# Where the maxima of w_out and the stored copies of w_in stand in the first mixer of a four-layer kernel

## The chip, the core and the metric

The kernel runs on one core of a Trainium2 chip. The metric is the device time of one execution in microseconds; a version's time is the median of its runs. Five engines work side by side, each through its own list of instructions in order: TensorE (PE; its weight loads are shown apart as PEld), VectorE (DVE), ScalarE (ACT), GpSimd (POOL) and SyncE (SP), which issues every DMA here. They wait for each other through semaphores.

## The reference

x is 2048 x 640. Two layers alternate twice: an attention with a compressive memory (A, 32 heads, four segments), and a gated mixer (B) over 2048 positions. Only B of the first pair is touched by the change.

```python
x = x + A(layernorm(x), wq, wk, wv, wo, beta)
x = x + B(layernorm(x), w_in, w_sp, b_sp, w_out)
x = x + A(...)          # the same weights again
x = x + B(...)

def B(x, w_in, w_sp, b_sp, w_out):          # w_in 640 x 1728, w_sp 2048 x 2048, w_out 864 x 640
    z = gelu(x @ w_in)
    z1, z2 = z[:, :864], layernorm(z[:, 864:])
    g = w_sp @ z2 + b_sp[:, None]
    return (z1 * g) @ w_out
```

## The kernel before

Matrix products are made in float16 with every factor split into a high and a low part, so each product is three matmuls (high x high, high x low, low x high). A factor is scaled by a power of two taken from its largest element before it is split; that needs its maximum first.

One layer pair runs in three phases. Phase 1a is the attention. Phase 1b (`phase1b`) makes z1 and z2 of the mixer, 16 row tiles of 128 positions. Phase 2 (`phase2`; `phase2s` in the second pair) makes the spatial product with w_sp and the output.

**Phase 1b of the first pair.** The loop runs over an index i = 0 to 15; index i handles row tile `ts[i]`, in the order 0 to 7, 12 to 15, 8 to 11. The attention's output projection of tiles 0 to 11 is done in phase 1a; tiles 12 to 15 are projected here (`attn_out`, line 311, tile `yp`), at the head of indices 7 to 10, one index ahead of their use, from a transposed tile `o` (line 299). For each tile x is normalised, split into high and low halves (`xnhl`) and turned by a transposing DMA into `th` (line 252). PE multiplies `th` with the second half of w_in (`wi1`, giving z2) and then with the first half (`wi0`, giving z1), 30 matmuls each (`zp`, line 334). z2 is normalised and split into `zh`, `zl`, which stay on the chip; z1 goes to DRAM (line 348). There are two buffers of `th`, so a tile's `th` is issued soon after PE has finished the tile two before it, and has to be there one tile later.

**What else the loop carries.** `keep()` (line 148) stores the split halves of w_in to DRAM for the second pair, two DMAs of 1080 KB for `wi1` and two for `wi0`. The generator `more` (`other_scales`, lines 203 to 222) finds the maximum of w_out: seven loads (`wmst`), seven reductions (`wap`), a reduction to one column (`wam`), its store (`wmax`), a load that broadcasts it (`wmall`) and a last reduction (`pw`). One `next(more)` takes one such step; twelve end it. Both stand behind that index's z2 norm on DVE and its z1 store on SP (`issue_after`), nothing else ties them.

**Phase 2.** Row tile t of w_sp is loaded (`wr`, one buffer, line 678), its row maxima found (`am`, line 684), scaled and split by column halves (`wn`, lines 700 and 701), turned by two transposing DMAs into `wt` (line 702) and multiplied with `zh`, `zl` (`gp`, line 713, 96 matmuls, from row tile 0 on, with the tiles of the last indices last). The product is gated with z1 (`cz`), scaled, split and turned (`un`, `ut`) and multiplied with w_out (`cyp`, line 745, called a tail here), one product later. PE's order is product 0, product 1, tail 0, product 2, tail 1 and so on. The loads and splits of w_out (`wst`, `wuh`, `wul`, lines 130, 90, 91) stand on ACT and DVE ahead of the first gate. The row tiles 0 and 1 are prepared ahead of the loop: `behind(10)` to `behind(14)` put their DVE and ACT steps behind the z2 of indices 10 to 14.

**What sets the order.** In phase 1b only PE's order is that of the code; a scheduler places the other engines' instructions, by priority and by when the buffers they need come free. The buffers of phase 2 lie where those of phase 1b lay: that of `wr` over buffers of x, `o` and the staging tiles of w_out's maxima. From the loop of `phase2` on, the order of PE, SP, DVE and ACT is that of the code.

Of the kernel before, what the change touches and what calls it, by code (L numbers as in the profile page):

```python
# [267 lines left out]
def phase1b(g, o_d, x, x1_d, z1_d, put, after, w0=None):  # L268
    nc, tc = g.nc, g.tc
    zs = ZS if w0 is None else ZB  # L270
    with ExitStack() as ctx:
# [18 lines left out]
        def load(t):  # L290
            if t < NWO:
                x1 = pe2.tile([128, D], F32, tag="x1", name="x1")
                nc.sync.dma_start(x1, x1_d[t])
                return (x1,)
            xt = px2.tile([128, D], F32, tag="xt", name="xt")
            nc.sync.dma_start(xt, x[t])
            o = px1.tile([128, 2, KD, 128], F16, tag="o", name="o")
            d = o_d[t // 4][(t % 4) * 128:(t % 4 + 1) * 128]
            nc.sync.dma_start(o.rearrange("p i k c -> p (i k) c"), d.rearrange("p i c -> p (i c)"), transpose=True)
            return xt, o[:, 0], o[:, 1]  # L300

        def attn_out(t, *a):
            if t < NWO:
                x1 = a[0]
            else:
                xt, oh, ol = a
                yp = py.tile([128, 2, 512], F32, tag="yp", name="yp")
                for k in range(KD):
                    for j, (a, b) in enumerate(((oh, woh), (oh, wol), (ol, woh))):
                        for n in range(2):  # L310
                            nc.tensor.matmul(yp[:, n, :320], a[:, k, :], b[:, k, n * 320:(n + 1) * 320],
                                             start=(k == 0 and j == 0), stop=(k == KD - 1 and j == 2))
                x1 = pe2.tile([128, D], F32, tag="x1", name="x1")
                nc.vector.scalar_tensor_tensor(x1.rearrange("p (n c) -> p n c", n=2), yp[:, :, :320], g.yw,
                                               xt.rearrange("p (n c) -> p n c", n=2), ALU.mult, ALU.add)
                nc.sync.dma_start(x1_d[t], x1)
            xn = x1 if t < NWO else xt
            layernorm(g, x1, xn, D, 2, XS)
            return xn

        def xn_t(xn):
            th = pe2.tile([128, 2, KD, 128], F16, tag="th", name="th")
            hl = pe1.tile([128, 2, D], F16, tag="xnhl", name="xnhl")
            split_t(g, hl, th, xn)
            return th[:, 0], th[:, 1]

        def w_in_half(i, th, tl):
            zp = (pz0, pz1)[i].tile([128, 2, 512], F32, tag=f"zp{i}", name=f"zp{i}")
            wh, wl = wi[i]
            for k in range(KD):  # L330
                for j, (a, b) in enumerate(((th, wh), (th, wl), (tl, wh))):
                    for n in range(2):
                        c = n * FHH
                        nc.tensor.matmul(zp[:, n, :FHH], a[:, k, :], b[:, k, c:c + FHH],  # L334
                                         start=(k == 0 and j == 0), stop=(k == KD - 1 and j == 2))
            return zp

        def z2_half(t, zp):
            z2 = p1.tile([128, FH], F32, tag=f"z2{t % 2}" if w0 is not None else "z2", name="z2")
            i = nc.scalar.activation(z2.rearrange("p (n c) -> p n c", n=2), zp[:, :, :FHH], AF.Gelu_apprx_tanh, scale=g.zi[1])  # L340
            j = layernorm(g, z2, z2, FH, 2, zs)
            put(t, z2, p1)
            return i.ins, j.ins

        def z1_half(t, zp):
            z1 = p2.tile([128, FH], F32, tag="z1", name="z1")
            nc.scalar.activation(z1.rearrange("p (n c) -> p n c", n=2), zp[:, :, :FHH], AF.Gelu_apprx_tanh, scale=g.zi[0])
            return nc.sync.dma_start(z1_d[t], z1).ins
# [16 lines left out]
        for i, t in enumerate(ts):  # L365
            if i + 1 < NT:
                xn = attn_out(ts[i + 1], *a)
            last = z2_half(t, w_in_half(1, *th))
            g.mark[i] = last
            if i + 2 < NT:  # L370
                a = load(ts[i + 2])
            th1 = xn_t(xn) if i + 1 < NT else None
            sent = z1_half(t, w_in_half(0, *th))
            th = th1
            with tc.issue_after(last[1]), tc.issue_after(sent):
                if w0 is None and i in (3, 6):
                    g.wi[i == 3].keep()
                if i > 2:
                    next(more, None)


# [1193 lines left out]
def interleaved_layers(ctx, tc, x, wq, wk, wv, wo, beta, w_in, w_sp, b_sp, w_out, out):  # L1575
# [25 lines left out]
    for i in range(2):  # L1601
        z1_d = [dram(f"z1_{i}_{t}", (128, FH)) for t in range(NT)]
        with ExitStack() as zs:
            with ExitStack() as top:
                phase1a(g, att[i], top)
                if i:
                    ats.close()
                    w0 = zs.enter_context(tc.tile_pool(name="w0", bufs=1, reuse_waits="tile")).tile([128, 2, 7 * D], F16, name="w0")
                zp = zs.enter_context(tc.tile_pool(name="z2", bufs=1, reuse_waits="tile"))
                if i:  # L1610
                    zb = [zp.tile([128, 2, NT // 2, FHH], F16, name=f"zb{j}") for j in range(7)]
                    phase1b(g, o_d[i], xs[i], x1_d[i], z1_d, blocks(g, zb), att[i].after, w0)
                else:
                    zh = zp.tile([128, NT, FH], F16, name="zh")
                    zl = zp.tile([128, NT, FH], F16, name="zl")
                    phase1b(g, o_d[i], xs[i], x1_d[i], z1_d, whole(g, zh, zl), att[i].after)
            if i:
                phase2s(g, w_sp, x1_d[i], z1_d, zb, w0, xs[i + 1])
            else:
                phase2(g, w_sp, x1_d[i], z1_d, zh, zl, xs[i + 1], att[1])  # L1620
# [26 lines left out]
```

## Time and profile before

| what | before |
|---|---|
| median of 3 runs | 2313.51 us (2311.42 to 2315.06) |
| profiled execution, its own time | 2322.67 us |
| span in that profile | 2321.0 us |
| PE busy | 2169.7 us (93%) |
| DVE, ACT, POOL busy | 1506.6, 1175.5, 973.9 us |
| DMA queue of SP | 347.19 MB, 57.1% of 16 engines' span |
| mean granted clock of PE | 0.983 |

The profile records one execution; its times are used below as durations and places, and they are counted from the span's start. The first pair's phase 1b runs from about 639 to 837 us, its phase 2 from 839 to about 1250 us. In a row of the timeline stand start, duration, engine, source line, operation, written and read tiles, count, and in brackets how long the engine had sat idle before it and what ended that.

### The profile page before, as it was taken

The numbers are of one execution on the slowest core, as the hardware profiler recorded it, in microseconds if no ns is written. First come the engines' busy times: TensorE is split into PE (matmuls) and PEld (weight loads), VectorE is DVE, ScalarE is ACT, GpSimd is POOL, SyncE is SP. The second block draws the span as 40 slices with busy tenths as digits, with TensorE's granted clock in tenths as the row PEclk, the third lists the DMA queues.
The fourth block names the chain that finished last, engine by engine and source line by source line (L and its number), as shares of the span: only waits on it lengthen the run. The fifth ranks groups of instructions, "written<-read, shape, count | busy, mean of one in ns | idle before, by whom it ended". The sixth has DMA issues, their size and how long they took to land.

```text
span 2321.0 us, 50425 instructions
## 1 busy us (share of the span) xinstructions
PE 2169.7 (93%) x20487; PEld 1296.1 (56%) x20487; DVE 1506.6 (65%) x2812; ACT 1175.5 (51%) x1462; POOL 973.9 (42%) x726
## 2 busy tenths in 40 slices
PE   4889899999899979999999988999998999999999
PEld 2455565656555535555654555656665555555555
DVE  7588878787744545454434788787776767546454
ACT  3388788787632222121113797888875434322321
POOL 2188788888610100000001688889896323000000
PEclk9999999999899989999999999999999999999999
DMA  5543635455655357878656336354456434877875
GB/s 162 146 102 106 165 91 131 109 157 125 162 146 163 105 156 203 243 182 223 189 145 160 70 97 168 86 125 120 124 162 176 108 95 110 248 220 195 224 212 127
DMA packets 512008, 350.41 MB, mean 151 GB/s; under 512 B 409952, under 2 KB 447712, under 8 KB 506656
## 3 DMA queue, kind: packets, MB, share of 16 engines
q1 hardware_dynamic: 511776, 347.19, 57.1%
q8 instruction: 160, 2.62, 0.5%
q14 instruction: 72, 0.59, 0.1%
HBM read 161.10 MB, written 97.93 MB: 112 GB/s over the span
## 4 chain that ended last, share of the span: by engine, by line
PE 49%; DVE 4%; ACT 4%; DMA 2%; issue 2%; POOL 1%; SPq 0%; ACTq 0%; DVEq 0%; POOLq 0%
PE gp L713 11%; PE zp L334 7%; PE cyp L548 3%; PE cyp L745 3%; PE ga L499 3%; PE gb L499 3%; PE vps L1094 2%; PE pv L1370 2%; PE yps L1127 2%; PE ge L499 2%; PE gd L499 2%; PE gc L499 2%; PE kps L1151 1%; PE mp L1317 1%; PE qps L1151 1%
## 5 line engine op out<-in xcount | busy, mean ns | idle before, releaser
L1344 POOL TENSOR_TENSOR PL<-P,PH 128x1280 f16<-128x1280 f32 x248 | 649.9, 2623 | 159.9 <-ACT PH L1343 144.6
L1333 DVE TENSOR_REDUCE mx<-mp 128x2 f32<-128x1024 f32 (+3 forms) x512 | 408.4, 817 | 95.1 <-PE mp L1289 92.8
L1326 ACT ACTIVATE P<-es,sc 128x1024 f32<-128x1024 f32 (+1 forms) x384 | 370.4, 965 | 126.4 <-PE es L1289 123.3
L1343 ACT CAST PH<-P 128x1280 f16<-128x1280 f32 x256 | 320.3, 1253 | 18.5 <-PE pv L1370 11.8
L238 POOL TENSOR_TENSOR lnrs<-lnve,mhalf 128x1 f32<-128x1 f32 x92 | 56.0, 618 | 586.9 <-DVE lnve L237 585.7
L334 PEld LDWEIGHTS <-th 128*128 128x128 f16 x1920 | 188.1, 98 | 170.3 <-DMA th<-xnhl 6.5
L713 PE MATMUL gp<-zh,wt 128*128 128x432 f16 x1024 | 233.4, 348 | 12.6 <-DMA wt<-wn 12.6
L713 PEld LDWEIGHTS <-wt 128*128 128x128 f16 x1536 | 150.7, 98 | 144.3 <-DMA wt<-wn 14.2
L1317 PEld LDWEIGHTS <-qk 60*128 60x128 f16 (+1 forms) x2048 | 91.9, 93 | 224.4 <-issue 161.5
L499 PEld LDWEIGHTS <-wt 128*128 128x128 f16 x1344 | 131.5, 98 | 112.6
L1317 PE MATMUL es<-qk 64*128 64x512 f16 (+3 forms) x1024 | 134.9, 299 | 41.4 <-ACT P L1326 29.1
L1317 PE MATMUL mp<-qk 60*128 60x512 f16 (+3 forms) x1024 | 137.6, 306 | 34.1 <-DVE mx L1333 32.7
L1289 PEld LDWEIGHTS <-big 64*128 64x128 f16 x3072 | 141.2, 95 | 49.8 <-issue 2.5
L1370 PE MATMUL pv<-vs,PH 128*128 128x41 f16 x2560 | 168.2, 182 | 0.1
L1370 PE MATMUL pv<-vs,PL 128*128 128x41 f16 x2560 | 163.9, 181 | 4.0 <-POOL PL L1344 3.7
L1094 PE MATMUL vps<-wvh,xt 128*128 128x320 f16 x640 | 152.1, 303 | 4.5 <-DVE vs L1100 3.5
L334 PE MATMUL zp<-wi1h,th 128*128 128x432 f16 x640 | 149.5, 349 | 6.5 <-DMA th<-xnhl 5.2
L1370 PEld LDWEIGHTS <-PH 128*128 128x128 f16 x2560 | 142.5, 96 | 18.4
L1370 PEld LDWEIGHTS <-PL 128*128 128x128 f16 x2560 | 142.9, 96 | 5.7 <-POOL PL L1344 4.6
L713 PE MATMUL gp<-zl,wt 128*128 128x432 f16 x512 | 136.1, 348 | 0.0
L1151 PE MATMUL kps<-xt,wkh 128*128 128x512 f16 x380 | 121.9, 388 | 7.6 <-DVE phl L1185 7.3
L726 DVE TENSOR_TENSOR u<-u,cz 128x864 f32<-128x864 f32 x16 | 17.0, 1060 | 161.7 <-ACT u L724 111.8
(260 smaller groups left out, 4389.8 us busy)
## 6 DMA issues: line engine op xcount, KB each, us to landing
wr<-in_B_w_sp_dram SPq DMA_DIRECT2D x32, 1024.0 KB
qk<-st SPq DMA_DIRECT2D x256, 120.0 KB
x<-x SPq DMA_DIRECT2D x56, 320.0 KB
z<-z SPq DMA_DIRECT2D x32, 432.0 KB
cz<-z SPq DMA_DIRECT2D x32, 432.0 KB
turned<-wt SPq DMA_DIRECT2D x24, 512.0 KB
wt<-turned SPq DMA_DIRECT2D x24, 512.0 KB
st<-qhl SPq DMA_DIRECT2D x40, 256.0 KB
```

The source lines that it names most:

```text
L334: nc.tensor.matmul(zp[:, n, :FHH], a[:, k, :], b[:, k, c:c + FHH], start=(k == 0 and j == 0), stop=(k == KD - 1 and j == 2))
L499: nc.tensor.matmul(o[:, :FHH], wt[:, x, m, :], zb[b][:, y, m, :], start=start and i == j == 0, stop=i == NP - 1 and j == 2, skip_group_che ...
L713: nc.tensor.matmul(gp[:, n, :FHH], ready[t][:, k % 2, a, k // 2, :], b[:, k, n * FHH:(n + 1) * FHH], start=(i == 0 and j == 0), stop=(i == ...
L1094: nc.tensor.matmul(ps, a[:, k, c], b[:, k, n * 320:(n + 1) * 320], start=(i == 0), stop=(i == 14))
L1151: nc.tensor.matmul(ps, a[:, k, c], b[:, k, :], start=(i == 0), stop=(i == 14))
L1289: nc.tensor.matmul(out, g.big[r, 64 - 64 * s:192 - 64 * s], mk, start=False, stop=s == 1, skip_group_check=True)
L1317: nc.tensor.matmul(out[:, h, o:o + w], a[r, ac], b[r, bc], start=o == 0, stop=False, skip_group_check=True)
L1326: self.last_of["ACT"] = nc.scalar.activation(P[:, :, 512 * c:512 * c + ew], es[:, :, :ew], AF.Exp, scale=g.esc).ins
L1333: self.last_of["DVE"] = nc.vector.tensor_reduce(self.mx[m][:, :, i], mp[:, :, o:o + w], AX.X, ALU.max).ins
L1343: nc.scalar.copy(PH, P[:, h])
L1344: (nc.gpsimd if h == 0 or n < self.N - self.TAIL else nc.vector).tensor_tensor(PL, P[:, h], PH, ALU.subtract)
L1370: nc.tensor.matmul(pv[:, i, h, :], x[:, c:c + 128], v[:, j, h0 + h, :], start=(j == 0 and x is PH), stop=(j == i and x is PL), skip_group_ ...
```

## The change

Three lines at the end of the loop of `phase1b`, which act in the first pair alone (`w0 is None`; in the second pair `more` is empty).

```diff
             with tc.issue_after(last[1]), tc.issue_after(sent):
-                if w0 is None and i in (3, 6):
-                    g.wi[i == 3].keep()
-                if i > 2:
+                if w0 is None and i in (7, 9):
+                    g.wi[i == 7].keep()
+                for _ in range(1 + (i == 7)):
                     next(more, None)
```

The store of `wi1` goes from index 3 to index 7, that of `wi0` from index 6 to index 9. The steps of w_out's maxima start at index 0 instead of 3, with two of them at index 7, so that they end at index 10 instead of 14. No instruction is added or removed, and PE's order is the same in both.

The scheduler follows these lines with others. On SP, the store of `wi1` stood here before (`z_0_3` is the DRAM copy of z1 of row tile 3; the `th` is that of index 5):

```order
L348 DMA z_0_3<-z_11628 128x864
L148 DMA w_i1h<-wi1h 128x4320
L148 DMA w_i1l<-wi1l 128x4320
L203 DMA wmst<-in_B_w_out_dram 128x640
L252 DMA_TRANSPOSE th<-xnhl 128x10x128
L293 DMA x_11788<-x_0_7 128x640
```

and it stands here now, behind z1 of row tile 7 (index 7); the `o` is that of row tile 14:

```order
L348 DMA z_0_7<-z_12069 128x864
L148 DMA w_i1h<-wi1h 128x4320
L148 DMA w_i1l<-wi1l 128x4320
L299 DMA_TRANSPOSE o<-o_3 128x10x128
L316 DMA x_0_13<-x_12108 128x640
L252 DMA_TRANSPOSE th<-xnhl 128x10x128
```

The store now has an `o` and the stored x of an output projection behind it before the next `th`.

Also on SP, the end of phase 1b before, with the first loads of w_sp (z1 of row tiles 9, 10 and 11 are those of indices 13, 14 and 15):

```order
L348 DMA z_0_9<-z_12760 128x864
L220 DMA wmall<-wmax 128x128
L252 DMA_TRANSPOSE th<-xnhl 128x10x128
L678 DMA wr<-in_B_w_sp_dram 128x2048
L348 DMA z_0_10<-z_12855 128x864
L702 DMA_TRANSPOSE wt<-wn 128x16x128
L348 DMA z_0_11<-z_12939 128x864
```

and the first two loads of w_sp now (z1 of row tiles 14, 15 and 8 are those of indices 10, 11 and 12):

```order
L678 DMA wr<-in_B_w_sp_dram 128x2048
L348 DMA z_0_14<-z_12473 128x864
L252 DMA_TRANSPOSE th<-xnhl 128x10x128
L293 DMA x_12632<-x_0_10 128x640
L348 DMA z_0_15<-z_12574 128x864
L252 DMA_TRANSPOSE th<-xnhl 128x10x128
L293 DMA x_12728<-x_0_11 128x640
L702 DMA_TRANSPOSE wt<-wn 128x16x128
L348 DMA z_0_8<-z_12670 128x864
L252 DMA_TRANSPOSE th<-xnhl 128x10x128
L678 DMA wr<-in_B_w_sp_dram 128x2048
L702 DMA_TRANSPOSE wt<-wn 128x16x128
```

The first `wr` has moved from behind the z1 store of index 13 to ahead of that of index 10, and the second `wr` and the second `wt` of row tile 0 now stand ahead of the z1 store of index 13 and of the `th` of index 15, which follow the last row shown.

On DVE, index 13 before (its z2 norm, the x norm for index 15, the low halves of both):

```order
L244 TENSOR_SCALAR z_12708<-z_12708,lnmv,lnrs 128x864
L244 TENSOR_SCALAR x_12722<-x_12722,lnmv,lnrs 128x640
L386 TENSOR_TENSOR zl<-z_12708,zh 128x864
L251 TENSOR_TENSOR xnhl<-x_12722,xnhl 128x640
L235 BN_STATS lnst<-z_12810 128x6 x2
```

and the same index now:

```order
L244 TENSOR_SCALAR z_12714<-z_12714,lnmv,lnrs 128x864
L701 SCALAR_TENSOR_TENSOR wn<-wr,wiv,wn 128x1024
L244 TENSOR_SCALAR x_12728<-x_12728,lnmv,lnrs 128x640
L386 TENSOR_TENSOR zl<-z_12714,zh 128x864
L251 TENSOR_TENSOR xnhl<-x_12728,xnhl 128x640
```

A split of w_sp's first row tile has come between the two norms. In the same way the row maxima of row tile 0 stand in index 11, its first split in index 12, the maxima and both splits of row tile 1 in index 14, ahead of the z2 norm of index 15.

## The prediction

> **What bounds the kernel now.** I read the page first, for the engine that sets the end, then the span cut at the starts of the mixer's tiles, then TensorE's waits in time order, then the DMA queue (SP) and VectorE around each wait.
>
> ```profile
> PE 49%; DVE 4%; ACT 4%; DMA 2%; issue 2%; POOL 1%; SPq 0%; ACTq 0%; DVEq 0%; POOLq 0%
> L713 PE MATMUL gp<-zh,wt 128*128 128x432 f16 x1024 | 233.4, 348 | 12.6 <-DMA wt<-wn 12.6
> L334 PE MATMUL zp<-wi1h,th 128*128 128x432 f16 x640 | 149.5, 349 | 6.5 <-DMA th<-xnhl 5.2
> ```
>
> The chain that ended last is mostly TensorE (PE). PE waits little, but two of its groups name a transposing DMA: 12.6 us before the spatial products (`gp`, waiting for `wt`) and 5.2 us before the mixer's input projections (`zp`, waiting for `th`). The change touches the work around exactly these. I cut the first layer's mixer at the tile starts; the columns are window, length, then busy us of PE, PEld, DVE, ACT and POOL with instruction counts, PE's granted clock, DMA share and GB/s.
>
> ```profile
> 682.63:696.56 13.93, 11.12 (x62) 5.78 (x60) 6.61 (x14) 4.68 (x6) 1.35 (x2) 1.00 0.84 256
> 696.56:709.20 12.64, 12.64 (x61) 6.42 (x61) 4.49 (x11) 2.22 (x3) 1.35 (x2) 0.86 0.31 93
> 709.20:720.15 10.95, 10.95 (x62) 5.87 (x60) 5.59 (x11) 3.78 (x5) 0.55 (x1) 1.00 0.38 102
> 720.15:735.20 15.05, 15.05 (x92) 8.83 (x91) 7.52 (x15) 3.60 (x4) 1.10 (x2) 1.00 0.91 285
> 802.30:814.92 12.62, 10.96 (x62) 5.68 (x59) 6.53 (x13) 3.64 (x5) 1.35 (x2) 1.00 0.24 62
> 825.90:839.22 13.32, 11.09 (x61) 5.76 (x60) 8.06 (x14) 4.79 (x5) 0.55 (x1) 1.00 0.30 74
> 839.22:849.29 10.07, 1.27 (x6) 0.50 (x6) 3.23 (x2) 1.15 (x1) 0.15 (x1) 0.57 0.72 200
> 849.29:868.00 18.71, 18.70 (x90) 9.46 (x91) 6.04 (x11) 4.62 (x5) 0.00 (x0) 0.87 0.67 195
> ```
>
> An undisturbed tile takes 10.95 us with PE busy throughout (third row), 15.05 with an output projection (fourth). The other rows carry an excess, and PE's own timeline says what each waited for:
>
> ```profile
> 696.56 0.54 PE L334 MATMUL zp<-wi1h,th 128*128 128x432 f16 x2 [2.81 <-DMA th<-xnhl]
> 814.92 0.54 PE L334 MATMUL zp<-wi1h,th 128*128 128x432 f16 x2 [1.66 <-DMA th<-xnhl]
> 849.29 0.90 PE L713 MATMUL gp<-zh,wt 128*128 128x432 f16 x2 [8.81 <-DMA wt<-wn]
> 885.69 0.43 PE L745 MATMUL cyp<-wuh,ut 128*128 128x320 f16 x2
> 892.82 0.54 PE L713 MATMUL gp<-zh,wt 128*128 128x432 f16 x2 [1.26 <-DMA wt<-wn]
> 894.38 0.54 PE L713 MATMUL gp<-zh,wt 128*128 128x432 f16 x2 [0.30 <-DMA wt<-wn]
> 910.99 5.71 PE cyp L745 x42
> 916.69 17.52 PE gp L713 x96
> 1218.21 17.52 PE gp L713 x96
> ```
>
> The last three rows are from the chain: a full-speed product is 17.52 us, a tail 5.71, and from 894.38 the chain runs over PE alone up to the last product at 1218.21. So whatever is won before 894 is handed on whole; no clocked event stands behind it.
>
> **The change, part by part.** (a) *The stores of w_in.*
>
> ```profile
> 684.92 0.43 SPq L148 DMA_DIRECT2D w_i1h<-wi1h  x1
> 687.31 2.81 SPq L252 DMA_TRANSPOSE th<-xnhl  x1
> 721.73 0.42 SPq L148 DMA_DIRECT2D w_i0h<-wi0h  x1
> 724.42 3.55 SPq L299 DMA_TRANSPOSE o<-o  x1
> 766.43 0.32 SPq L348 DMA_DIRECT2D z<-z  x1
> 774.76 1.33 SPq L252 DMA_TRANSPOSE th<-xnhl  x1
> ```
>
> At index 3 the store of `wi1` (two DMAs of 1080 KB) goes out at 684.92, ahead of the `th` of index 5. That `th` is issued at 687.31 and lets PE start at 696.56, 9.25 us later. The excess is (13.93 - 10.95) + (12.64 - 10.95) = 2.98 + 1.69 = 4.67 us; the second part is the tile at granted clock 0.86 after the wait. The same two DMAs for `wi0` at 721.73 (index 6) cost nothing: the tile behind them holds an output projection, and PE is busy for all of its 15.05 us at DMA share 0.91. The change puts both stores, at indices 7 and 9, in front of such tiles. At 7 the queue behind the store is that of 721.73 (`o`, x1, `th`) less one load of w_out. At 9 no `o` is left; the `th` behind it comes 774.76 - 766.43 = 8.3 us after the z1 store that the w_in store follows, more than the 2.4 us of 684.92 to 687.31. I take the whole **4.67** as gained, by the row at 720.15; the other end is nothing, if a store makes a `th` late again.
>
> [...]
>
> (b) *W_out's maxima.* Seven loads and seven reductions start at index 0 instead of 3, and the small store `wmax` moves from index 12 to 8.
>
> ```profile
> 708.51 0.81 DVE L206 TENSOR_REDUCE wap<-wmst 128x1 f32<-128x640 f32 x1
> 710.93 0.37 SPq L203 DMA_DIRECT2D wmst<-in_B_w_out_dram  x1
> 804.44 1.00 SPq L218 DMA_DIRECT2D wmax<-wam  x1
> 805.61 1.34 SPq L252 DMA_TRANSPOSE th<-xnhl  x1
> ```
>
> A load ahead of a `th` and a reduction of 0.81 us ahead of a norm stand in the tile 709.20 to 720.15, which is full with VectorE busy for 5.59 of 10.95 us; so I cost the move at nothing (without that cover at most 7 x 0.81 = 5.7 us; a gain is excluded, as these tiles have no wait to lose). The `th` of index 14, issued right behind `wmax`, lands 9 us later, and PE waits 1.66 us; the tile's excess is 12.62 - 10.95 = **1.67**. Behind the moved `wmax` stands an `o` that has a 15 us tile before it is needed. I take 1.67 as gained; ends 0 and 1.67.
>
> (c) *The first rows of w_sp.* This is the large part, though no line of it is in the diff. The first `wr` load leaves the end of the maxima's queue and goes to index 10.
>
> ```profile
> 781.62 0.32 SPq L348 DMA_DIRECT2D z<-z  x1
> 818.97 0.81 SPq L678 DMA_DIRECT2D wr<-in_B_w_sp_dram  x1
> 811.77 0.73 DVE L244 TENSOR_SCALAR z<-z,lnmv,lnrs 128x864 f32<-128x864 f32 x1 [0.60 <-POOL lnrs L238]
> 840.44 1.28 DVE L701 SCALAR_TENSOR_TENSOR wn<-wr,wiv,wn 128x1024 f16<-128x1024 f32 x1 [1.69 <-ACT wn L700]
> 841.75 0.33 SPq L678 DMA_DIRECT2D wr<-in_B_w_sp_dram  x1
> 842.13 15.09 SPq L702 DMA_TRANSPOSE wt<-wn  x3
> ```
>
> Before, it is issued at 818.97 and the second half's transpose only at 842.13, so the first product starts late and stops after six matmuls. After, it stands ahead of the z1 store at 781.62: 37 us earlier, some three tiles. Both halves of `wt` are then issued in indices 12 and 13, and the second row tile is split ahead of the last z2. What falls away: 13.32 - 10.95 = 2.37 before product 0; in products 0 and 1, from 839.22 to the tail at 885.69, 46.47 - 2 x 17.52 = 11.43 (8.81 idle, the rest at clock 0.57 and 0.87); before product 2, 892.82 - (885.69 + 5.71) = 1.42, and 0.30 inside it. Together **15.52**.
>
> *What is late next.* Product 2 needs row tile 2, whose scaling follows the first gate on VectorE and the seven splits of w_out on ScalarE.
>
> ```profile
> 858.39 13.01 SPq L130 DMA_DIRECT2D wst<-in_B_w_out_dram  x7
> 874.81 1.05 ACT L724 ACTIVATE u<-gp,bsp,un 128x864 f32<-128x864 f32 x1
> 888.76 5.58 DMA wt<-wn
> ```
>
> With 4.67 + 1.67 + 2.37 = 8.71 gone, product 0 starts at 839.22 - 8.71 = 830.51 and ends at 848.0. The splits took 874.81 - 858.39 = 16.4 us from their first load; now the loads run on from the last z1 store, near 832, so they end near 848.5. From the gate's first step to the transposed tile it was 888.76 + 5.58 - 874.81 = 19.5 us: ready at 868.0. Product 2 is due at 848.0 + 17.52 + 5.71 = 871.3, so 3 us are left and nothing is charged.
>
> *A new collision.* In index 13 `wr` of row tile 1 and `wt` of tile 0 now go out ahead of the `th` of index 15.
>
> ```profile
> 1943.46 4.47 DMA th<-xnhl
> ```
>
> The norm of index 13 ends at 812.50 - 4.67 = 807.8, the split 1.28 later, so `wr` goes at 809.1. From `wr` (841.75) to the product's restart (849.29) it was 7.54 us, so `wt` lands at 816.7. A `th` alone takes 4.47 in the second layer. Issued at about 812 beside the others it lands at 816.5, behind them at 821.1; it is due at 825.90 - 6.34 = 819.6. So it costs 0 to 1.6; I charge 0.9, nearer the queue's order, as 687.31 waited for what stood ahead.
>
> Sum: 4.67 + 1.67 + 15.52 - 0.9 = **21.0 us**. The profiled execution took 2322.67 (span 2321.0), so 2301.7 of its like; it stands 9.2 over the median of 2313.51, and as the terms are waits inside the kernel I take them off the median: **2292.5**.
>
> **Rivals.** *R1, the lines collide.* More than one `th` of indices 11 to 15 comes late behind the moved `wi0` store, `wr` and `wt`. For: 9.25 us at 687.31. Against: each of those tiles has only one large transfer more, and DMA shares there were 0.24 to 0.56. Two late ones at 4.67 give back 9.3: 2301.8. [...]
>
> *R2, the change does not bring `wr` forward*, because on the chip the load or its split is held by a buffer or by PE, or product 2's wait replaces product 0's. Then (c) is lost and 6.3 is left: 2307.2. Against: in the order the load stands between instructions that run at 774.76 and 781.62.
>
> *R3, slower.* The large transfers keep one `th` late in every tile from index 10 to 15 and each gap throws the clock down, at 4.67 a tile: 28.0 lost against 21.9 gained, 2319.7. It decides when five tiles pay (23.4). Place: the `zp` groups between 765 and 826. Against: the same queue took 2.2 MB at 721.73 with PE full.
>
> **How the numbers follow.** Forecast (gain of 18 to 22) 0.74; R1 0.14; R2 0.07; R3 0.03; four late `th` instead of two (18.7 given back, no change to be told) 0.02. The range goes from all of 21.9 gained with the runs' scatter of 2 us below the median (2289.5) to R1 (2302); it leaves out R2 and R3. A measurement of this kernel tells 0.2%, 4.6 us, from no change: faster 0.93, same 0.03, slower 0.04.
>
> **What would show it.** Right: no wait for `th` near 693, with a full tile there; `wr` issued near 770 to 775; product 0 directly behind the last `zp`; a chain over PE alone from about 830. Wrong: a `zp` wait above 2 us in indices 11 to 15 (R1, R3); 8 us or more before a `gp` in products 0 to 2 (R2); a late `o` ahead of the output projection of index 9 or 10 (a store whose cover is too short).

## The result and the profile after

| what | before | after |
|---|---|---|
| median, run side by side | 2314.28 us (2311.42 to 2318.5, 4 runs) | 2289.18 us (2288.19 to 2292.94, 4 runs) |
| ratio, 95% interval | | 0.9889 [0.9877, 0.9901] |
| profiled execution, its own time | 2322.67 us | 2288.19 us |
| span in that profile | 2321.0 us | 2286.5 us |
| PE busy | 2169.7 us | 2155.7 us |
| mean granted clock of PE | 0.983 | 0.991 |

The changed kernel is 25.1 us faster by these medians. Its page first: the shares of the chain that ended last, and the two groups that had named a transposing DMA.

```profile
PE 72%; DVE 9%; ACT 6%; DMA 4%; issue 3%; POOL 1%; SPq 0%; ACTq 0%; DVEq 0%; POOLq 0%
L713 PE MATMUL gp<-zh,wt 128*128 128x432 f16 x1024 | 231.2, 346 | 0.0
L334 PE MATMUL zp<-wi1h,th 128*128 128x432 f16 x640 | 148.1, 346 | 2.1 <-DVE x L1133 1.3
```

The idle time before `gp` is 0.0 where it was 12.6 us, and before `zp` 2.1 where it was 6.5; no DMA is named any more. The stretches of the first mixer, cut at the tile starts (columns as in the prediction: window, length, busy time by engine, granted clock, DMA share, GB/s):

```profile
684.37:695.32 10.95, 10.95 (x62) 5.87 (x61) 6.11 (x14) 3.39 (x5) 1.35 (x2) 1.00 0.36 100
721.32:736.37 15.05, 15.05 (x92) 8.83 (x91) 7.26 (x16) 3.60 (x4) 1.10 (x2) 1.00 0.86 265
799.40:810.40 11.00, 10.99 (x61) 5.74 (x60) 6.33 (x10) 3.63 (x6) 0.55 (x1) 1.00 0.82 213
810.40:821.30 10.90, 10.90 (x60) 5.83 (x61) 7.09 (x15) 5.03 (x5) 0.55 (x1) 1.00 0.55 131
```

The first row is index 5, whose `th` was late before. The second is the tile behind the moved store of `wi1`, at DMA share 0.86 and still full. The last two are indices 14 and 15. PE's timeline has one wait of 0.2 us or more between 629 and 900 us, 0.64 us at the mixer's first matmul, which the kernel before has too. The chain of work runs over PE alone from there:

```profile
629.62 76.81 PE zp L334 x420
...
755.58 54.75 PE zp L334 x300
810.34 11.12 PE zp L334 x60
821.47 35.04 PE gp L713 x192
856.51 5.71 PE cyp L745 x42
862.21 17.52 PE gp L713 x96
...
1186.96 17.52 PE gp L713 x96
```

Products 0 and 1 are one block of 35.04 us, twice 17.52. SP's queue shows the moved instructions at their new places:

```profile
722.87 0.42 SPq L148 DMA_DIRECT2D w_i1h<-wi1h  x1
725.56 4.59 SPq L299 DMA_TRANSPOSE o<-o  x1
...
737.89 0.43 SPq L218 DMA_DIRECT2D wmax<-wam  x1
740.59 1.32 SPq L299 DMA_TRANSPOSE o<-o  x1
...
752.92 0.42 SPq L148 DMA_DIRECT2D w_i0h<-wi0h  x1
...
764.16 0.38 SPq L678 DMA_DIRECT2D wr<-in_B_w_sp_dram  x1
...
799.83 0.33 SPq L678 DMA_DIRECT2D wr<-in_B_w_sp_dram  x1
800.21 5.43 SPq L702 DMA_TRANSPOSE wt<-wn  x1
...
806.37 1.48 SPq L252 DMA_TRANSPOSE th<-xnhl  x1
```

How much of the gain lies here is read from windows over the whole phase, of the kernel before and then of the changed one: first `zp` to first `gp`, products 0 and 1, the rest up to the end of the last product. The changed kernel's are cut where the chain has its steps; its first `gp` begins 0.17 us before the first of these cuts, so a part can be off by that much, the sum is not.

```profile
638.80:839.22 200.42, 193.69 (x1080) 105.95 (x1080) 98.45 (x204) 56.62 (x64) 19.29 (x31) 0.99 0.48 134
839.22:885.69 46.47, 37.66 (x193) 19.44 (x194) 20.02 (x31) 12.65 (x14) 0.15 (x1) 0.85 0.64 186
885.69:1235.73 350.04, 348.48 (x2085) 203.58 (x2084) 153.04 (x266) 67.55 (x72) 7.80 (x8) 1.00 0.75 196
sum 596.93, PE 579.84 PEld 328.98 DVE 271.51 ACT 136.81 POOL 27.24; mean PE 193.28 PEld 109.66 DVE 90.50 ACT 45.60 POOL 9.08
```

```profile
629.62:821.47 191.85, 191.84 (x1081) 105.69 (x1081) 102.70 (x213) 58.70 (x66) 20.37 (x31) 1.00 0.60 154
821.47:856.51 35.04, 35.04 (x194) 18.82 (x193) 16.18 (x24) 10.90 (x12) 0.15 (x1) 1.00 0.68 199
856.51:1204.48 347.97, 347.97 (x2084) 203.62 (x2083) 150.98 (x264) 67.11 (x71) 7.80 (x8) 1.00 0.73 195
sum 574.86, PE 574.85 PEld 328.12 DVE 269.87 ACT 136.71 POOL 28.32; mean PE 191.62 PEld 109.37 DVE 89.95 ACT 45.57 POOL 9.44
```

200.42 - 191.85 = 8.57, 46.47 - 35.04 = 11.43 and 350.04 - 347.97 = 2.07: together 22.07 us, and PE is busy in 574.85 of the 574.86 us that are left. The other 3 us of the 25.1 have to lie in parts of the program that the change doesn't touch, or in the runs' scatter: the ratio's interval allows a gain of 22.9 to 28.5 us.

### The profile page after: what moved, and what is told of

It is laid out like the page before. It is cut to its first block, busy times and chain, and to the rows that moved or that the text cites. A ratio compares the mean times of both kernels' runs of the same rounds, so it can differ in the third digit from the quotient of the medians.

```text
span 2286.5 us, 50423 instructions
## 1 busy us (share of the span) xinstructions
PE 2155.7 (94%) x20487; PEld 1290.6 (56%) x20487; DVE 1507.5 (66%) x2812; ACT 1174.7 (51%) x1462; POOL 972.8 (43%) x726
## 4 chain that ended last, share of the span: by engine, by line
PE 72%; DVE 9%; ACT 6%; DMA 4%; issue 3%; POOL 1%; SPq 0%; ACTq 0%; DVEq 0%; POOLq 0%
PE zp L334 15%; PE gp L713 12%; PE cyp L745 4%; PE pv L1370 4%; PE cyp L548 3%; PE vps L1094 3%; PE yps L1127 3%; PE ga L499 3%; PE gb L499 3%; DVE mx L1333 3%; PE mp L1317 3%; PE qps L1151 3%; PE kps L1151 2%; ACT P L1326 2%; ACT PH L1343 2%
## 5 line engine op out<-in xcount | busy, mean ns | idle before, releaser
L1343 ACT CAST PH<-P 128x1280 f16<-128x1280 f32 x256 | 320.3, 1253 | 19.7 <-PE pv L1370 11.4
```

The source lines that it names most:

```text
L1343: nc.scalar.copy(PH, P[:, h])
```

## The experiments

Theory: the three terms of the prediction are three separate things (the store ahead of a `th`, the small `wmax` store ahead of a `th`, the late first `wr`), each tied to its line of the diff. Rivals: the whole gain comes from the maxima, and the stores are hidden anyway; or the gain beyond 22 us is a fourth effect of the change. A ratio below is to the kernel before, run beside the experiment on the same chip, with its 95% interval. "Mixer" is the time from the start of the first `zp` to that of the first `gp` (191.7 us in the first profile of the changed kernel), "products" that of products 0 and 1.

**The two kernels again.** Unchanged copies of both.

> The kernel before, once more, for a second profile of it. Prediction's terms: again 8.7 us of waits and slow clock between the first zp and the first gp (191.6 us without them, 200.4 with them) and 13.2 us from there to the end of product 2. Theory 'scatter': the 3 us that the change gained beyond its phase (from the last gp of the first pair to the first zp of the second it was 3.25 us shorter) and the 9.2 us that the first attention was shorter are differences between executions: in this profile the first zp starts anywhere between 627 and 641 us, and the way from the last gp to the second pair's first zp is off by some us from 552.7. Theory 'carried on': the change itself shortens the second attention: then this profile has 552.7 within 0.5 us.

> The changed kernel, once more. 2289 by both theories (ratio 0.989); from the first zp to the first gp 191.6 to 191.8 us again. Theory 'scatter': from the last gp of the first pair to the first zp of the second somewhere in the span of the kernel before's profiles. Theory 'carried on': again 549.4, 3.25 us under the kernel before's.

Before: ratio 1.0003 [0.9989, 1.0016]. After: 2292.2 against 2316.8 us, ratio 0.9893 [0.9876, 0.9911]. The phases repeat closely: mixer 200.6 and products 46.3 us before, 191.5 and 35.0 after. The stretch ahead of the mixer does not: it took 638.8 and 629.4 us in the two profiles of the kernel before, 629.6 and 635.9 in those of the changed kernel, with the same instructions in all. The 23 runs of the kernel before beside these spread from 2310.37 to 2322.49 us.

**The maxima alone.** The stores stay at indices 3 and 6.

```diff
-                if i > 2:
+                for _ in range(1 + (i == 7)):
                     next(more, None)
```

> The maxima moved as in the change, the stores left at indices 3 and 6. By the prediction's terms 1.67 + 15.52 = 17.2 us of the gain: 2297.1 (ratio 0.9926); the wait for th at index 5 stays, 2.8 us and a slow tile behind it, 4.67 together; no wait before gp. Rival 'the stores do it': 2309.6 (0.998), with the wait before gp still there. Rival 'the early loads collide': the th of index 5 is later still than before, since the queue now carries a load of w_out in the tiles ahead: 2300 or more.

Ratio 0.9929 [0.9913, 0.9945]. PE's timeline and the windows at index 5, behind the store that stayed:

```profile
691.36 0.54 PE L334 MATMUL zp<-wi1h,th 128*128 128x432 f16 x2 [2.78 <-DMA th<-xnhl]
```

```profile
677.50:691.40 13.90, 11.12 (x62) 5.78 (x61) 7.68 (x16) 4.63 (x7) 1.35 (x2) 1.00 0.92 257
691.40:704.00 12.60, 12.60 (x60) 6.36 (x61) 4.48 (x11) 2.20 (x3) 1.35 (x2) 0.86 0.31 94
```

The excess over two tiles of 10.95 us is 2.95 + 1.65 = 4.60 us, where the kernel before had 4.67. The wait for `wt` is gone: products take 35.0 us. So the maxima carry `wr` forward, and the store's wait is a thing of its own.

**The stores alone.** The maxima still start at index 3.

```diff
-                if w0 is None and i in (3, 6):
-                    g.wi[i == 3].keep()
+                if w0 is None and i in (7, 9):
+                    g.wi[i == 7].keep()
```

> The stores moved as in the change, the maxima left from index 3 on. By the prediction's terms 4.67 us: 2309.6 (ratio 0.9980); full tiles up to index 12; the waits at index 14 (1.7 us) and before gp (2.2, 8.8, 1.6 us) stay. Rival 'the stores bring wr forward too': 2294 or less. Rival 'a store late behind index 9 makes a th wait, as a load of w_out stands behind it': above 2311, with a wait before zp at index 11.

Ratio 0.9983 [0.9970, 0.9997], 3.9 us of 2316.8. The mixer takes 195.5 us, 4.9 less than the 200.4 of the kernel before's first profile. PE's timeline keeps the waits for the `th` behind `wmax` and for `wt`; the longest of each:

```profile
806.83 0.36 PE L334 MATMUL zp<-wi1h,th 128*128 128x432 f16 x1 [1.48 <-DMA th<-xnhl]
...
841.37 0.54 PE L713 MATMUL gp<-zh,wt 128*128 128x432 f16 x1 [8.96 <-DMA wt<-wn]
```

This refutes the rival "the stores are hidden anyway", and it shows what R2 of the prediction would have looked like.

**The maxima late, but quick.** Stores at 7 and 9; the maxima start at index 3 and take two steps at each of 7 to 10, so that they end at 10 as in the changed kernel. If only their end matters, this must be as fast.

```diff
-                if i > 2:
+                for _ in range((i > 2) + (6 < i < 11)):
                     next(more, None)
```

> The stores as in the change; the maxima start at index 3 as before but take two steps at each of indices 7 to 10, so that they end at 10; wr goes out at index 11, one tile later than in the change. Theory 'the end of the maxima sets wr': the whole gain, ratio 0.989 to 0.990, no wait before gp, 191.6 us from the first zp to the first gp, 35.1 for products 0 and 1. Rival 'the early start matters': ratio 0.993 or more. Rival 'one tile less lead is too little': a wait before gp of 1 to 5 us.

A miss: 0.9928 [0.9907, 0.9948]. Products take 35.0 us, so the end of the maxima does decide `wr`, as expected. But the mixer takes 197.1 us. SP's queue and PE's wait say why:

```profile
761.29 0.51 SPq L148 DMA_DIRECT2D w_i0h<-wi0h  x1
761.85 0.46 SPq L148 DMA_DIRECT2D w_i0l<-wi0l  x1
762.41 1.14 SPq L218 DMA_DIRECT2D wmax<-wam  x1
...
769.24 1.33 SPq L252 DMA_TRANSPOSE th<-xnhl  x1
```

```profile
778.46 0.54 PE L334 MATMUL zp<-wi1h,th 128*128 128x432 f16 x1 [3.56 <-DMA th<-xnhl]
```

`wmax` has come to stand between the store of `wi0` and the `th` of index 11, which lets PE start 9.2 us after its issue, as it did behind `wmax` alone and behind the store alone before (9.31 and 9.25 us in the kernel before's first profile). It is `wmax` that does it: the changed kernel has the same store at this place, with the load `wmall` behind it instead of `wmax`, and no wait. The start at index 0 thus does a second thing: it puts `wmax` ahead of an `o`, not of a `th`.

**The maxima one index earlier than before.** Stores at 7 and 9 as in the change, maxima from index 2 with one step each, so that they end at index 13; `wmax` comes to index 11.

```diff
-                if i > 2:
+                if i > 1:
                     next(more, None)
```

> The stores as in the change; the maxima start at index 2, one index earlier than before: wmax goes out at index 11 and wr one tile (10.95 us) earlier than before. Theory: of the waits before gp (2.2, 8.9 and 1.3 us) the first is covered and of the second 11.2 - 10.95 = 0.3 us plus what the queue adds is left, so products 0 and 1 take 35 to 39 us together, not 46; ratio 0.990 to 0.993. wmax as cause of the wait of 1.5 to 1.75 us before zp at index 14: that wait now stands at index 13 (the th behind wmax). Rival 'the wait belongs to index 14': it stays at 14. The clock after the wait of 2.45 us some 31 us behind the last gp of the first pair: it fell in all three profiles with slow products and in none of the three others; if that follows from the slow products, it stays up here when products 0 and 1 run without a clock drop.

Ratio 0.9933 [0.9917, 0.9949]; the wait of term (b) moved with `wmax` from index 14 to index 13:

```profile
785.51 0.42 SPq L218 DMA_DIRECT2D wmax<-wam  x1
786.04 1.35 SPq L252 DMA_TRANSPOSE th<-xnhl  x1
```

```profile
796.17 0.36 PE L334 MATMUL zp<-wi1h,th 128*128 128x432 f16 x1 [1.85 <-DMA th<-xnhl]
```

The products lie between the two kernels, 38.6 us against 46.5 and 35.0: the first `wr` goes out at 800.94, 165 us after the mixer's start at 635.5, against 180 before and 134.5 after. PE now has three short waits in place of the long one, 0.65 us for `wt`, 2.53 us for `ut` at the first tail and 0.48 us for `wt` again.

**The store without cover.** As the change, but the store of `wi0` at index 12, where no output projection follows.

```diff
-                if w0 is None and i in (3, 6):
-                    g.wi[i == 3].keep()
-                if i > 2:
+                if w0 is None and i in (7, 12):
+                    g.wi[i == 7].keep()
+                for _ in range(1 + (i == 7)):
                     next(more, None)
```

> As the change, but the store of wi0 at index 12 instead of 9: the th of index 14 stands right behind it, in a tile without an output projection, and the second wr and wt behind that. Theory 'a store ahead of an uncovered th costs what it cost before': a wait before zp at index 14 of about 2.8 us and a slow tile, 4.7 us: ratio to the kernel before 0.991 (2294 against 2289 for the change). If the queue's backlog reaches the th of index 15 too, up to 9 us: 0.993. Rival 'the store is harmless in any tile now': 0.989, full tiles throughout.

Ratio 0.9923 [0.9908, 0.9939]. The mixer takes 196.7 us, 5.0 more than the changed kernel's 191.7, and one row has the cause:

```profile
793.80 0.43 SPq L148 DMA_DIRECT2D w_i0h<-wi0h  x1
794.28 0.77 SPq L148 DMA_DIRECT2D w_i0l<-wi0l  x1
795.16 4.39 SPq L252 DMA_TRANSPOSE th<-xnhl  x1
```

```profile
803.80 0.54 PE L334 MATMUL zp<-wi1h,th 128*128 128x432 f16 x2 [3.38 <-DMA th<-xnhl]
```

The same two DMAs cost 5.0 us at index 12 and nothing at index 9, so it is the tile behind them that hides them; the second `wr` and `wt` can't be the cause, as they are issued behind this `th`, from 800.87 on.

**Where the gain beyond 22 us is.** All profiles so far had the same wait of PE in the second attention, for the split of the first keys and queries: it begins 28 to 29 us behind the last product's end and is over some 31 us behind it. In the kernel before the granted clock fell behind it, in the changed one it did not. The wait in PE's timeline and the windows around it, before and then after:

```profile
1266.84 0.60 PE L1151 MATMUL kps<-xt,wkh 128*128 128x512 f16 x2 [2.46 <-DVE phl L1185]
```

```profile
1263.90:1267.30 3.40, 0.94 (x10) 0.53 (x10) 2.52 (x4) 1.53 (x3) 1.39 (x1) 1.00 0.72 223
1267.30:1270.70 3.40, 3.40 (x12) 1.02 (x12) 0.46 (x1) 0.72 (x1) 0.79 (x1) 0.50 0.73 187
```

```profile
1235.05 0.59 PE L1151 MATMUL kps<-xt,wkh 128*128 128x512 f16 x2 [2.42 <-DVE phl L1185]
```

```profile
1230.10:1233.50 3.40, 2.53 (x16) 1.09 (x15) 3.33 (x8) 0.72 (x1) 1.59 (x2) 1.00 1.06 321
1233.50:1236.90 3.40, 1.85 (x9) 0.78 (x8) 2.16 (x3) 1.28 (x2) 0.35 (x1) 1.00 0.76 184
```

Within one execution all changes of the granted clock lay, to 0.1 us, on a grid of 3.413 us (the 31 in the first profile of the kernel before, from 41.90 to 2322.00 us; the 13 in that of the changed kernel, from 42.27 to 2288.24). The windows above are grid windows. Before, the wait lies inside one of them and the next runs at 0.50; after, a boundary cuts it into 0.87 and 1.55 us and the clock stays at 1.00. Theory "grid": the cut belongs to the changed kernel and its place can be computed. Rival "scatter": it comes and goes by chance. Three kernels repeat the first matmul of product 8 (each repetition is overwritten by the next, so it only takes time), to shift the wait against the grid:

```diff
             gp = pg.tile([128, 2, 512], F32, tag="gp", name="gp")
+            for _ in range(7 * (t == 8)):
+                nc.tensor.matmul(gp[:, 0, :FHH], ready[t][:, ks[0] % 2, 0, ks[0] // 2, :], zh[:, ks[0], :FHH], start=True, stop=True)
             for i, k in enumerate(ks):
```

with 7 and 14 in the changed kernel, and 12 in the kernel before.

> The changed kernel with 7 more matmuls (the first one of the product repeated, each overwritten by the next) ahead of product 8 of the first pair: they cost 7 x 17.52 / 96 = 1.28 us on PE and shift everything behind by that much against the clock's 3.41 us grid. Theory 'grid': in the changed kernel the 2.42 us wait of PE 31 us behind the last product (1232.63 to 1235.05) is cut by a grid boundary at about 1233.5 and the clock stays at 1.00. Shifted by 1.28 the wait lies inside one grid window (from 0.4 to 2.9 us of 3.41), so the clock falls to half behind it: the 40 us behind the last product at clock 0.95 to 0.97, the stretch from the last product to the second pair's first zp 557 to 558.7 instead of 555.3 to 555.9, total 1.28 plus 1.7 to 3.4 above the changed kernel (ratio to before about 0.9910). Rival 'scatter' (the drop comes and goes by chance with the execution): only 1.28 above, ratio about 0.990, and no rule for the clock behind the wait.

> The same with 14 more matmuls, 2.55 us. Grid: the shifted wait is cut again by a boundary (1.7 and 0.7 us on its sides), so the clock stays at 1.00 behind it, the stretch is 555.3 to 555.9, and the total is 2.55 above the changed kernel: no slower than with 7 more matmuls, though PE does 1.28 us more. Scatter: 1.28 above the kernel with 7 more.

> The kernel before with 12 more matmuls there, 2.19 us. Grid: its wait (1264.38 to 1266.84, inside the window 1263.9 to 1267.3) moves to 2.7 us of its window and is cut into 0.7 and 1.7, so the drop that all profiles of this kernel showed behind it goes away: the stretch from the last product to the second pair's first zp 555.3 to 556.5 instead of 558.1 to 558.5, and the total 0.5 below to 0.2 above the kernel before, ratio 0.9998 to 1.0001. Scatter: drop as before, ratio 1.0009.

> The changed kernel once more. Grid: no drop behind the wait at 31 us, the stretch 555.3 to 555.9 for the third time, ratio to before 0.9890 to 0.9900, and 22.0 us gained between the mixer's first zp and the last product as in both profiles so far. Scatter: a drop as likely as not.

The last column is the stretch from the start of the last product's last matmul to the second pair's first z1 matmul (`zp<-w`), in the one profile of each run.

| run | time, us | ratio to before | wait cut into, us | clock behind it | that stretch, us |
|---|---|---|---|---|---|
| after, 7 more | 2295.8 | 0.9913 [0.9900, 0.9927] | 1.07, 1.23 | 1.00 | 556.1 |
| after, 14 more | 2299.52 | 0.9935 [0.9918, 0.9952] | 1.52, 0.90 | 1.00 | 556.8 |
| before, 12 more | 2320.5 | 1.0019 [1.0008, 1.0030] | 2.45 whole | falls | 559.0 |
| after again | 2292.19 | 0.9901 [0.9886, 0.9915] | 1.80, 0.59 | 1.00 | 557.0 |

The steering failed: with 7 more the wait was to be whole and was cut, with 12 more it was to be cut and was whole. The reason is in the same profiles. A slow window ahead of the wait holds about half the work (in the kernel before 11 matmuls at clock 0.50 from 697.28 to 700.69 us, 21 at 1.00 in the next window; the tile with the slow one took 12.64 us instead of 10.95), and so moves everything behind it by about 1.7 us, half a window; the profile with 7 more had one at 628.1 to 631.5 that the first profile of the changed kernel hadn't, and that with 12 more had three slow windows around products 0 and 1 (836.6 to 846.9) where the kernel before had four. In all four the clock still went with the cut: it fell behind the wait that was whole (2.45 us in one window) and stayed at 1.00 behind the three that were cut (at most 1.80 us in one window). The times can't decide either: with 14 more the median is 7.3 us above "after again", where 2.55 us of work were added, and its profile is of the fastest of its four runs, so it doesn't show where the rest went. Two more profiles of each kernel were to tell whether the cut is chance:

> A further profile of the kernel before. If the 1.7 us of clock behind the wait at 31 us after the last product belong to this kernel, the wait lies again inside one grid window (over 2.0 us of it in one) and the clock falls, stretch to the second pair's first zp 557.5 to 559; if its place on the grid is chance, a cut wait with the clock at 1.00 is as likely.

> A further profile of the changed kernel. If it belongs to this kernel: the wait is cut again, at most 1.85 us of it in one window, clock at 1.00, stretch 555 to 557; if chance: a drop is as likely. Between the mixer's first zp and the last product 22.0 to 22.2 us less than before either way.

> As for e12_before_look2: a drop behind the wait if it belongs to the kernel, a cut wait with the clock at 1.00 as likely if it is chance.

> As for e13_after_look2: a cut wait and no drop if it belongs to the kernel, a drop as likely as not if it is chance.

The kernel before lost the clock in both (2.17 and 2.28 us of the wait in one window; the stretch of the table 559.6 and 562.4 us), the changed kernel in neither (1.88 and 1.80 us; 557.1 and 556.0). From the mixer's first `zp` to the start of the last product's last matmul it was 596.5 and 596.7 against 574.4 and 574.6 us, 22.1 us less each time.

## Why the prediction came out as it did

2289.18 us were measured, 0.3 below the range's low end of 2289.5 and 3.3 below the forecast of 2292.5. The sum was right for the mixer, 21.0 us net against 22.07, and too small for the whole program by the 3 us that lie elsewhere; the kernel before ran 0.8 us slower beside it than the median used, which took that much off the miss. The two later medians of the changed kernel, 2292.2 and 2292.19, lie on the forecast, but by luck: the kernel before ran at 2316.8 and 2315.95 beside them, 3.3 and 2.4 us above the 2313.51 from which the forecast was reckoned, and that hides a gain that was again larger than 21.0.

- **The stores, 4.67.** Right in place and size: alone they bring 4.9 us in the mixer, left where they were they cost 4.60, and taken from their cover 5.0. The second part, the tile at lower clock behind the wait, came back each time.
- **W_out's maxima, 1.67, and their move at nothing.** Right: the wait follows `wmax` (index 14 with the stores alone, 13 in the kernel with the maxima from index 2) and is gone where `wmax` has an `o` behind it. The reductions in the earlier tiles cost nothing: those tiles are full. (The reduction that the prediction shows, at 708.51, lies in the tile before the one it names; another of 0.81 us at 718.81 lies in it, so the reading holds.)
- **The first rows of w_sp, 15.52.** Right: counted from the mixer's start, the first `wr` goes out at 764.16 - 629.62 = 134.5 us, which is 773.4 on the kernel before's scale (forecast: near 770 to 775). Products 0 and 1 gave 11.43 as worked out, the two ends 2.23 (8.57 less 4.67 and 1.67) and 2.07 where 2.37 and 1.72 were put. Product 2 didn't wait, as its margin of 3 us said.
- **The new collision, 0.9.** Not paid. The second `wr` went out 170.2 us into the mixer, as forecast (809.1 - 638.8 = 170.3), and the `th` of index 15 at 806.37, later than thought; but PE took it up at 810.40 without a wait, so it landed in at most 4.03 us beside a `wt` that was issued ahead of it. "Nearer the queue's order" was the wrong choice between the bounds.
- **Rivals.** R1 (late `th`) showed itself in the kernel with the uncovered store, with one late tile, and in the one with the quick maxima; R2 (product 2, or no earlier `wr`) in the stores alone, where 3.9 us were left (R2's 6.3 less the 1.67 of `wmax`, which had not moved there, would be 4.7). R3 nowhere.

So the mixer gave 22.07 us where the three terms came to 21.86; the charge of 0.9 was the larger of the two errors in it.

**The step that failed** is "whatever is won before 894 is handed on whole; no clocked event stands behind it". One does: the wait at 1264.38 to 1266.84 us and the clock's grid behind it. In four of four profiles of the kernel before it cost a slow window, 3.41 / 2 = 1.71 us; in five of five of the changed kernel it cost none. The stretch in which it lies took 558.1 to 562.4 us before and 555.3 to 557.1 after. Three medians put the whole gain at 25.1, 24.6 and 23.8 us, so 1.7 to 3.0 lie outside the mixer, where the prediction had put nothing. By these medians alone that is hardly clear of the noise (the last two intervals reach down to 20.6 and 19.7 us); what shows it is the profiles.

The link to the change is arithmetic, not an experiment: in the kernel before, the last slow stretch is the one at products 0 and 1, it ends on a boundary (854.2, 844.8, 848.6 and 853.7 us in the four profiles), and the wait begins 409.3 to 410.1 us later, 120 windows of 3.413 us being 409.6; PE is idle for 1.4 to 2.0 us in between. So the wait begins within 0.5 us of a boundary, and over 2.1 us of it lie in one window. This hangs on where in its window product 0 goes on: with 12 more matmuls the slow stretch ended only 3.2 us behind that, not 4.9 to 5.6, and the wait began 413.5 us later, 1.2 to 2.0 more than the added 2.2 us explain. In the changed kernel that stretch is gone, and the wait begins 1.5 to 2.8 us into a window in all five profiles. At a place taken at random, about half of all places leave 2.07 us or more of such a wait in one window (an estimate from its 2.42 us and the window's 3.413), so nine of nine by chance would be rare, but the tries to move the wait on purpose didn't succeed.

What fills the gap between 1.71 us and the mean difference of the stretch, 559.7 - 556.3 = 3.4, is in part other slow windows: between the last product and the drop that all nine have ahead of the second mixer (1728 us or later), the kernel before had 1, 2, 4 and 3 in its four profiles, the one behind the wait among them, the changed kernel 0, 0, 2, 2 and 1. Whether the change has a share in these others is open.

**The range** had a second fault. Its low end (2313.51 - 21.86 - 2 = 2289.65, put as 2289.5) took "the runs' scatter of 2 us" from three runs. The kernel before spreads over 12 us in 23 runs. Much of that arises ahead of the mixer, in work that is the same in both kernels: it took from 629.4 to 638.8 us in the nine profiles of the two, with 8 slow windows in the shortest and 15 in the longest, though not in proportion (13 at 631.4 and at 637.8).

## What to carry to other kernels

When a large store must go out, put it ahead of the tile with the most work left before the next thing queued behind it; the same transfer cost 5 us at one index here and nothing three indices earlier. Read a removed wait together with the slow clock behind it, and look in the rest of the program, even in code that the change doesn't touch, for waits of about the length behind which the clock fell here (2.07 us or more in one window of 3.41): the wait of some 2.4 us in the second attention, with the same instructions in both kernels, was followed by a slow window in four of four profiles of one and in none of five of the other. Take a range's scatter from many runs, or from what the profiles of one kernel lose to the clock, not from three times that happen to lie close.

## What the hardware showed that was not expected

**The clock's grid.** In each of 17 profiles the changes of the granted clock lay on a grid of 3.413 us, whose origin differs from one execution to the next (the first changes at 41.90 and 42.27 us in the first profiles of the two kernels). From the mixer's start to 1270 us a window at full clock that held at most 2.00 us of PE's idle time left the clock at 1.00 (the wait of 1.85 us in the kernel with the maxima from index 2; 2.00 of a wait of 2.25 us ahead of product 0 in the kernel with the stores alone), and one that held 2.07 us or more was followed by a window at 0.50 (the least: 2.07, of the 2.60 us wait at index 5 in the third profile of the kernel before). So in this stretch 2.07 of 3.41 us, about 60% of one window, was enough, and the second attention's wait of 2.30 to 2.47 us cost its own length and then 1.71 us or nothing, by where it fell. Two limits: a window already at 0.50 was followed by another at 0.50 with less idle time (1.2 to 2.0 us, once in each of the four profiles of the kernel before, where product 0 went on), and in the attentions, where the matmuls have other shapes, 1.67 us were enough in one window (kernel before, 233.05 to 236.46) and 1.80 us were not in another (changed kernel, 1550.96 to 1554.37).

**A small store that holds up a transpose.** `wmax` is 512 bytes. The next `th` behind it let PE start some 9 us after its issue in the kernel before and 9.2 in that with the quick maxima, though in the kernel before the DMA engines moved nothing from 810 us on (windows of that kernel):

```profile
810.00:812.00 2.00, 2.00 (x12) 1.07 (x11) 1.40 (x7) 0.00 (x0) 0.81 (x2) 1.00 0.00 0
812.00:814.00 2.00, 1.26 (x7) 0.49 (x5) 1.58 (x3) 0.91 (x1) 0.53 (x1) 1.00 0.00 0
```

The transfers that the trace records had ended by 810, some 5 us before PE could go on at 814.92. The trace also records the semaphore updates by which a DMA tells that it has landed, 16 for each one named here. Those of `wmax` came between 808.05 and 812.98, those of the `th` behind it between 810.50 and 814.87, though its last packet had ended at 808.5; twelve other `th` of this mixer had their last update 3.3 to 5.3 us after the issue, and the one behind the store of `wi1` 9.2. In the changed kernel `wmax` is as slow, from 742.10 to 747.91, and the `o` behind it lands 8.9 us after its issue, at 749.46; the tile of 15 us hides it. So what comes late here is the word that the data has landed, for `wmax` and for the transposes behind it. Why is open: no run separated the size of the store from its kind or its place.
